# A scan and a gated MLP on one core: a table made on the chip, and another order of the first loads

## The chip, the cores and the metric

The kernel runs on one NeuronCore of a Trainium2 chip. The metric is device time in microseconds (us) of one execution. The core has five engines with instruction streams of their own: TensorE (PE in the profile, with its weight loads as PEld), VectorE (DVE), ScalarE (ACT), GpSimd (POOL) and SyncE (SP), which here only issues DMAs. Each engine works through its stream in order and waits on semaphores for the others. DMAs are carried out by 16 DMA engines that all queues share.

## The reference

Two stages. The first is a causal linear attention with decays, for 4 batches, 8 heads, 768 positions, head size 32 and state size 16; the second is a gated MLP on the 3072 resulting rows of 256.

```python
log_a = np.log(np.clip(a, 1e-06, 1.0))
for c in range(nc):                                   # chunks of the sequence
    cum = np.cumsum(la, axis=-1)
    L = np.exp(cum[:, :, :, None] - cum[:, :, None, :]) * causal
    M = np.einsum('bhin,bhjn->bhij', Cc, Bc) * L
    y_intra = np.einsum('bhij,bhjd->bhid', M, xc)
    y_inter = np.einsum('bhin,bhnd->bhid', Cc, state) * np.exp(cum)[:, :, :, None]
    state = decay_full * state + sum over j of Bc * xc * decay_from_j
g = x @ w_gate                                        # (3072, 256) @ (256, 1536)
out = (g * (1.0 / (1.0 + np.exp(-g))) * (x @ w_val)) @ w_out
```

## The kernel before, in words

**Blocks.** The sequence is cut into NB = 6 blocks of 128 positions, each of K = 2 pieces of Q = 64. A block holds T = 512 rows of the MLP (4 batches by 128). Block by block, the attention gives y, which is the input x of the MLP; TensorE then runs the gate and value products (tile gv, 12 column pieces f of 128) and later the sums over the hidden size (tile po).

**Decay tables.** L[j, i] is the product of decays from position j to position i. It is made on VectorE by a scan along i: state = state * a + d, where d is a table with a one at i = j, which starts the product. This diagonal table is the tile dj, 128 partitions (j, twice 64) by 8 heads by W = 65. dn is the like table for E, the decays from the start of a piece. For block 0 the decays come as 8 rows (load_rows), are clipped on VectorE (clip_rows), spread over 128 partitions by TensorE matmuls with a table pick (spread, tile a), and scanned from PSUM (scan_spread). For later blocks all decays are loaded once (load_all), clipped on GpSimd (clip_all), written to DRAM (write_all, tile clipped) and read back as broadcasts (load_aj into L, load_an into E).

**Attention of a block.** heads_apart makes Cz from C on ScalarE or VectorE with masks hm out of the constants cs; scores (tile S) are matmuls of B and Cz; mix multiplies L by S on VectorE; weigh_first and weigh_b multiply B, which lies beside x in the tile xb, by the last column of L; sums gives the states (tile st), apart puts them into T; values and carried give y; weigh_c multiplies C by E. For block 0, x_whole copies y to the tile xf.

**Weights.** The weights come as float64 bit patterns, 18 pieces of 512 KB (12 of gate and value, wg0 to wg11, then 6 of the output, wo0 to wo5), and are turned into float32 on the chip: w_magnitude and w_rest on ScalarE, w_range on GpSimd (on VectorE for pieces 1 and 2), then w_shift, w_sign and w_round on VectorE. The raw pieces lie in 8 buffers (RAW = 8, tag wraw), which the hidden tiles hh use too; a buffer comes free when its piece is rounded. In block 0 the products use the rounded piece as float32; for later blocks w_high, w_minus and w_low split it into two parts.

**The order.** Nothing but the opening statements (from load_rows to the fills of dn) is in hand order. All else is an operation in a list: add(engine, cost, run, rank, needs, takes, uses, gives, lag). A planner (class Plan) runs through modelled time at build time: on each engine it takes, among the operations that can start first, the one of lowest rank. What it finds is the program order of each engine. lag is the modelled transfer time of a load, needs are operations that must come before, and follow(list) fixes an order of issue. ScalarE and VectorE are chosen by the planner where both are given with a cost. The plan's times only decide the order; on the chip engines wait on semaphores.

In the plan before, the raw pieces 2 and 3 are issued behind the scores of block 0, 4 and 5 behind mixes 1 and 3, and 7 behind y of block 0. VectorE's opening order is fixed as the scans of block 0, mixes 0 to 2, the weighing of B (bt), mix 3, E, the weighing of C (ce) and the sign step of piece 0.

All engine calls go through a helper (class Ordered), so every operation of the profile has the line L191; they are told apart by their tiles.

## Time and profile before

| | |
|---|---|
| median of 3 runs | 351.83 us (351.35 to 351.98) |
| the profiled execution | 352.14 us, its span 350.3 us |
| TensorE busy | 342.8 us, 98% of the span |
| VectorE busy | 231.3 us, 66% |
| ScalarE busy | 121.9 us, 35% |
| GpSimd busy | 46.0 us, 13% |
| DMA | 31.28 MB, mean 89 GB/s |
| first gate and value product of block 0 | starts at 16.89 us |

How to read it: rows of a timeline give the start in us, the busy time in us, engine, line, operation, output tile <- input tiles, shape and count (xN are N instructions merged), and in brackets the idle time ahead of it with what ended it. SPq, ACTq and POOLq are DMA issues; the time of such a row is that of the issue, not of the transfer. A row of the DMA view gives a load, its queue, its size and the median us from issue to landing. A row of the waits gives total us, times, longest. A row of the windows gives the stretch, its length, the busy time and count of PE, PEld, DVE, ACT and POOL, the granted TensorE clock, the DMA share and GB/s. Busy time of a matmul is modelled at its end, so neighbours overlap in the rows.

### The profile page before, as it was taken

To read this page: it belongs to the slowest core of one execution; us is meant where nothing else is said; L and a number is where in the kernel's file an instruction comes from. 1 tells how busy PE (TensorE), PEld (TensorE's weight loads), DVE (VectorE), ACT (ScalarE), POOL (GpSimd) and SP (SyncE) were. 2 spreads that over 40 slices of the span, in tenths; PEclk is the share of its full clock that TensorE was granted. 3 is DMA by queue.
4 is the path that set the end of the run, shared out by engine and by line. 5 is a ranking of instruction groups with operands and counts; after the bars stand their busy time and mean duration, and the time that the engine had idled before them with its cause. 6 is when DMAs were issued, how large, how long until landed. Compare 5 with 4: busy or idle time off the path is not lost.

```text
span 350.3 us, 7386 instructions
## 1 busy us (share of the span) xinstructions
PE 342.8 (98%) x3183; PEld 265.6 (76%) x3184; DVE 231.3 (66%) x415; ACT 121.9 (35%) x221; POOL 46.0 (13%) x36
## 2 busy tenths in 40 slices
PE   7999989999999999999999999999999999999996
PEld 5644445688878888878888878888888888888895
DVE  4999999998689774686447677456676430565320
ACT  3599677434355512212222222221212221222221
POOL 1374884402301000000000000000000000000000
PEclk9999999999999999999999999999999999999999
DMA  7799998850000751000382000281000000100001
GB/s 258 241 318 309 334 277 185 225 120 2 1 2 4 204 158 62 0 2 2 111 175 82 0 2 2 84 199 59 24 3 2 2 2 0 60 2 0 0 2 60
DMA packets 10216, 31.28 MB, mean 89 GB/s; under 512 B 1184, under 2 KB 2080, under 8 KB 9544
## 3 DMA queue, kind: packets, MB, share of 16 engines
q1 hardware_dynamic: 8136, 26.77, 25.4%
q0 software_dynamic: 1728, 3.15, 5.0%
q10 hardware_dynamic: 320, 0.89, 0.8%
q8 instruction: 25, 0.41, 0.5%
q14 instruction: 7, 0.06, 0.1%
HBM read 24.32 MB, written 3.35 MB: 79 GB/s over the span
## 4 chain that ended last, share of the span: by engine, by line
PE 92%; DVE 3%; issue 1%; ACT 0%; DVEq 0%; ACTq 0%
PE gv L191 57%; PE po L191 28%; PE y L191 5%; PE S L191 2%; DVE wg8w L191 1%; DVE L L191 1%; DVE wg0w L191 1%; DVE E L191 0%; DVE wg7w L191 0%; DVE sg L191 0%; DVE xb L191 0%; ACT ob L191 0%; DVE bc L191 0%; DVEq L191 0%; ACTq L191 0%
## 5 line engine op out<-in xcount | busy, mean ns | idle before, releaser
L191 DVE TENSOR_TENSOR sg<-gv,sg 128x512 f32<-128x512 f32 x72 | 49.5, 688 | 66.5 <-PE gv L191 65.3
L191 ACT ACTIVATE sg<-gv 128x512 f32<-128x512 f32 x72 | 43.1, 598 | 109.7 <-PE gv L191 109.6
L191 DVE TENSOR_TENSOR hh<-sg,hh 128x512 fp32r<-128x512 f32 x72 | 49.5, 691 | 16.0 <-ACT hh L191 14.6
L191 ACT CAST hh<-sg 128x512 fp32r<-128x512 f32 x36 | 22.3, 623 | 31.1 <-PE po L191 17.5
L191 DVE TENSOR_TENSOR_SCAN L<-L,dj 128x520 f32<-128x520 f32 x20 | 23.9, 1228 | 5.8 <-DMA L<-clipped 5.8
L191 ACT COPY ob<-po 128x512 f32<-128x512 f32 (+1 forms) x13 | 7.2, 555 | 48.6 <-PE po L191 48.2
L191 DVE CAST hh<-sg 128x512 fp32r<-128x512 f32 x36 | 15.8, 438 | 1.2
L191 PE MATMUL po<-hh,wo4h 128*128 128x512 f32 (+1 forms) x52 | 15.2, 375 | 0.0
L191 PE MATMUL po<-hh,wo2h 128*128 128x512 f32 (+1 forms) x52 | 15.2, 375 | 0.0
L191 PE MATMUL po<-hh,wo0h 128*128 128x512 f32 (+1 forms) x52 | 15.2, 375 | 0.0
L191 DVE TENSOR_TENSOR L<-S,L 128x512 f32<-128x512 f32 x24 | 15.1, 678 | 0.0
L191 PE MATMUL po<-hh,wo5h 128*128 128x512 f32 (+1 forms) x52 | 15.1, 373 | 0.0
L191 PE MATMUL po<-hh,wo1h 128*128 128x512 f32 (+1 forms) x52 | 15.0, 373 | 0.0
L191 PE MATMUL po<-hh,wo3h 128*128 128x512 f32 (+1 forms) x52 | 15.0, 373 | 0.0
L191 PEld LDWEIGHTS y<-L,xb 64*32 64x32 f32 x768 | 9.6, 111 | 3.1 <-issue 1.8
L191 PE MATMUL y<-L,xb 64*32 64x64 f32 x768 | 11.9, 239 | 0.0
L191 PEld LDWEIGHTS po<-hh,wo0h 128*128 128x128 f32 x52 | 9.5, 188 | 1.9 <-issue 0.2
L191 PEld LDWEIGHTS po<-hh,wo5h 128*128 128x128 f32 x52 | 9.5, 188 | 1.7
L191 PEld LDWEIGHTS po<-hh,wo1h 128*128 128x128 f32 x52 | 9.5, 188 | 1.7
L191 PEld LDWEIGHTS po<-hh,wo3h 128*128 128x128 f32 x52 | 9.5, 188 | 1.7
L191 PEld LDWEIGHTS po<-hh,wo2h 128*128 128x128 f32 x52 | 9.4, 188 | 1.8
L191 PEld LDWEIGHTS po<-hh,wo4h 128*128 128x128 f32 x52 | 9.4, 188 | 1.7
(304 smaller groups left out, 756.0 us busy)
## 6 DMA issues: line engine op xcount, KB each, us to landing
L<-clipped SPq DMA_DIRECT2D x10, 520.0 KB, 10.7
xb<-in_xb SPq DMA_DIRECT2D x5, 768.0 KB, 13.8
bc<-in_bc SPq DMA_DIRECT2D x6, 512.0 KB, 4.4
out<-ob SPq DMA_DIRECT2D x11, 256.0 KB, 2.0
E<-clipped SPq DMA_DIRECT2D x5, 260.0 KB
xb<-in_xb ACTq DMA_DIRECT2D x1, 768.0 KB, 6.3
wg0r<-in_wgv SPq DMA_DIRECT2D x1, 512.0 KB
wg1r<-in_wgv SPq DMA_DIRECT2D x1, 512.0 KB
```

What stands on the lines that cost most here:

```text
L191: ins = getattr(self.engine, name)(*a, **k)
```

## The change

**The table dj** is no longer copied from the constants. Two iotas on GpSimd (one for each 64 partitions) write i - j into a new tile step_of, and one VectorE instruction compares it with 0 into dj. Both stand ahead of the other opening work of their engines' planned order: the iotas ahead of the fills of unit and dn, the compare ahead of the clipping of the rows. The constants cs shrink by 65 columns of 131 (from 65.5 KB by half).

**The loads.** x and B of block 0 (load_xb) go out on SP behind C and B (load_bc) where they went out on ScalarE's queue. The raw pieces lose their needs on scores, mixes and y. A new list ORDER fixes the order of issue on SP: piece 7, the write of the clipped decays, piece 8, block 1's bc, aj and xb, piece 9, block 1's an, piece 10. The modelled lags of several loads change.

**The order of VectorE's opening** now puts the weighing of B ahead of all four mixes, and the rounding of piece 0 behind its sign step. All four copies x_whole are ScalarE's. The rest step of piece 3 comes behind the last of them.

```diff
--- before.py
+++ after.py
@@ -219,7 +219,8 @@
     ps_at = pool("ps_at", 4, space=PSUM)
 
     cs = const.tile([P, CST], F32, name="cs")
-    eye, hm, blk = cs[:, 0:W], cs[:, W : W + 2], cs[:, W + 2 : W + 2 + 2 * D]
+    hm, blk = cs[:, :2], cs[:, 2 : 2 + 2 * D]
+    step_of = const.tile([P, W], F32, name="step")
     pick = const.tile([64, BATCH + 1, P], F32, name="pick")
     dj = const.tile([P, H, W], F32, name="dj")
     dn = const.tile([P, BATCH * K, W], F32, name="dn")
@@ -285,7 +286,7 @@
     def load_xb(k):
         t = bl[k]["xb"] = att.tile([P, BATCH, DM + P], F32, tag="xb", name=f"xb{k}")
         bl[k]["x"], bl[k]["Bj"] = t[:, :, :DM], t[:, :, DM:]
-        (sp if k else se).dma_start(t, xb[k])
+        sp.dma_start(t, xb[k])
 
 
     def clip(t):
@@ -664,7 +665,7 @@
 
         if not i:
             rest[n] = ps_at.tile([P, 512], F32, tag="at", name=f"rest{n}")
-        times, wide = (4, 64) if not n else (1, 512)
+        times, wide = ((4, 64), (1, 512))[n]
         for _ in range(times):
             te.matmul(rest[n][:, :wide], unit[:, :P], unit[:, :wide], start=True, stop=True)
 
@@ -678,6 +679,12 @@
     load_all()
     ve.memset(warm, 1.0)
     se.activation(warm, warm, AF.Silu)
+    for q in range(K):
+        ge.iota(
+            step_of[piece(q)], pattern=[[1, W]], base=0, channel_multiplier=-1,
+            allow_small_or_imprecise_dtypes=True,
+        )
+    ve.tensor_scalar(dj, step_of.unsqueeze(1).to_broadcast([P, H, W]), 0.0, None, ALU.is_equal)
     ge.memset(unit[:, P:], 1.0)
     ge.memset(dn, 0.0)
     ge.memset(dn[:, :, :1], 1.0)
@@ -709,7 +716,6 @@
         return begin_sum[k] + f * PO
 
     add("-", 0.0, lambda: None, -9, gives="pick", lag=0.1)
-    add([("Act", 0.6), ("DVE", 0.6)], None, lambda e: copy(e, dj, eye.unsqueeze(1).to_broadcast([P, H, W])), -8.5, ["cs"], gives="dj")
     add("-", 0.0, lambda: None, -8, gives="cs", lag=0.4)
 
 
@@ -722,12 +728,12 @@
 
     for i in range(NW):
         r = due(0, i) - 1.0 if i < NF else due_sum(0, 2 * (i - NF)) - 1.0
-        add("SP", 0.48, do(w_fetch, i), r - 9.0, [("S", 0, BATCH - 1)] if i in (2, 3) else [("M", 0, 2 * i - 7)] if i in (4, 5) else [("y", 0)] if i == 7 else [], takes=[("raw", ("raw", i))], gives=("raw", i), lag=2.1)
+        add("SP", 0.48, do(w_fetch, i), r - 9.0, takes=[("raw", ("raw", i))], gives=("raw", i), lag=1.3)
         add("Act", 0.57, do(w_magnitude, i, "Act"), r - 5.5, [("raw", i)], takes=[("sg" if i < NF else "w", ("w", i))], gives=("mag", i))
         far = not 0 < i < 3
         e, c = ("Pool", 2.2) if far else ("DVE", 0.335)
         add(e, c, do(w_range, i, ge if far else ve), r - 4.5, [("mag", i), *([("round", i - 1)] if i == 1 else [])], gives=("range", i))
-        add("Act", 0.57, do(w_rest, i, "Act"), r - 4.5, [("raw", i)], gives=("rest", i))
+        add("Act", 0.57, do(w_rest, i, "Act"), r - 4.5, [("raw", i), *([("xf", 3)] if i == 3 else [])], gives=("rest", i))
         add("DVE", 0.335, do(w_shift, i), r - 4.2, [("range", i)], gives=("shift", i))
         add("DVE", 0.6, do(w_sign, i), r - 3.9, [("shift", i)], gives=("sign", i))
         add("DVE", 0.6, do(w_round, i), r - 3.3, [("sign", i), ("rest", i)], uses=[("raw", i)], gives=("round", i))
@@ -744,7 +750,7 @@
 
     add("-", 0.0, lambda: None, -7.9, gives="all", lag=0.9)
     add("Pool", 1.0, clip_all, -9, ["all"], gives="clipped")
-    add("SP", 0.48, write_all, -9, ["clipped"], gives="written", lag=0.9)
+    add("SP", 0.48, write_all, -9, ["clipped"], gives="written", lag=1.5)
 
 
     for k in range(NB):
@@ -764,8 +770,8 @@
         def load(f):
             return do(f, k) if k else lambda: None
 
-        add(*q, load(load_bc), FETCH["bc"] if k == 1 else z - 7 if k else -7.7, late + behind("bc") + loaded, takes=[("bc", BC)], gives=("bc", k), lag=2.1)
-        add(*q, load(load_xb), FETCH["xb"] if k == 1 else z - 6 if k else -6, late + behind("xb") + loaded, takes=[("xb", XB)], gives=("xb", k), lag=3.1)
+        add(*q, load(load_bc), FETCH["bc"] if k == 1 else z - 7 if k else -7.7, late + behind("bc") + loaded, takes=[("bc", BC)], gives=("bc", k), lag=1.3)
+        add(*q, load(load_xb), FETCH["xb"] if k == 1 else z - 6 if k else -6, late + behind("xb") + loaded, takes=[("xb", XB)], gives=("xb", k), lag=1.9)
         if not k:
             add("-", 0.0, lambda: None, -9, takes=[("x", "rows")], gives="rows", lag=0.2)
             for i in range(3):
@@ -775,12 +781,12 @@
                 for i in range(2 if b < BATCH else 1):
                     t = ("spread", b, i)
                     add("PE", 0.25 if first(b, i) else 0.45, do(spread, b, i), r + 0.5 * i, [("clip", b % 2 if b < BATCH else 2), "pick"], takes=[("mm" if first(b, i) else "at", t)], uses=[t, "rows"], gives=t, kind="s")
-                    need = [t, ("decays", 0), "dj"] + ([("scan0", b)] if i else [])
+                    need = [t, ("decays", 0)] + ([("scan0", b)] if i else [])
                     done = ("E", 0) if b == BATCH else ("L", 0, b) if i else ("scan0", b)
                     add("DVE", 0.63, do(scan_spread, b, i), r + 0.5 * i, need, uses=[t], gives=done)
         else:
             add("SP", 0.96, do(load_aj, k), FETCH["aj"] if k == 1 else z - 12, ["written", ("decays", k), *late], gives=("aj", k), lag=4.3)
-            add("SP", 0.48, do(load_an, k), FETCH["an"] if k == 1 else z - 9, ["written", ("decays", k), *late], gives=("an", k), lag=1.1)
+            add("SP", 0.48, do(load_an, k), FETCH["an"] if k == 1 else z - 9, ["written", ("decays", k), *late], gives=("an", k), lag=2.4)
             for b in range(BATCH):
                 add("DVE", 1.14, do(scan_j, k, b), z + 0.5 + b, [("aj", k)], gives=("L", k, b), slack=1.0)
             add("DVE", 1.17, do(scan_n, k), z + 6, [("an", k)], gives=("E", k), slack=1.0)
@@ -830,7 +836,7 @@
         if not k:
             add("-", 0.0, new_whole, -9, [("clip", 2)], takes=[("x", "xf")], gives="xf")
             for i in range(2 * K):
-                add([("Act", 0.36)] if i < 3 else [("Act", 0.36), ("DVE", 0.36)], None, do(x_whole, i), -1 + i / 10, [("vals", i) if i < 2 else ("y", 0), "xf", *([("round", 0)] if i == 3 else [])], uses=[y[i]], gives=("xf", i))
+                add([("Act", 0.36)], None, do(x_whole, i), -1 + i / 10, [("vals", i) if i < 2 else ("y", 0), "xf"], uses=[y[i]], gives=("xf", i))
             continue
         add("-", 0.0, do(new_x, k), z + 15, [("x", k - 1)] if k > 1 else ["xf"], takes=[("x", ("x", k))], gives=("x", k))
         for i in range(2 * K):
@@ -878,18 +884,20 @@
         ("spread", BATCH, 0), *(("st", 0, b) for b in range(BATCH)),
     ])
     plan.follow([("raw", i) for i in range(NW)])
-    plan.follow([("L", 0, b) if i else ("scan0", b) for b, i in halves] + [("M", 0, p) for p in range(3)] + [("bt", 0)] + [("M", 0, 3), ("E", 0), ("ce", 0), ("sign", 0)])
+    plan.follow(ORDER)
+    plan.follow([("L", 0, b) if i else ("scan0", b) for b, i in halves] + [("bt", 0)] + [("M", 0, p) for p in range(NP)] + [("E", 0), ("ce", 0), ("sign", 0), ("round", 0)])
     plan.STAY = {"Act": 0.0, "PE": 0.3}
     plan.issue()
 
 
-CST = W + 2 + 2 * D
+CST = 2 + 2 * D
 NA = NB * K * BATCH * H // P
 IDLE = [-9.0] * 6, [0.5, 1.0]
 IDLE_AFTER = [], [("y", 0)]
 FETCH = dict(aj=10.0, an=35.0, bc=12.0, xb=31.0)
 LATER = 3.0
 PAGE = 4.4
+ORDER = [("raw", 7), "written", ("raw", 8), ("bc", 1), ("aj", 1), ("xb", 1), ("raw", 9), ("an", 1), ("raw", 10)]
 LEAD = {1: -30.0, 2: -44.0, 3: -44.0}
 LATE = {2: NF + 2}
 
@@ -922,10 +930,9 @@
 
     p = np.arange(P)
     cst = np.zeros((P, CST), np.float32)
-    cst[:, :W] = (p % Q)[:, None] == np.arange(W)[None, :]
     odd = (p // N) % 2
-    cst[:, W : W + 2] = odd[:, None] == np.arange(2)[None, :]
-    cst[:, W + 2 : W + 2 + 2 * D] = odd[:, None] == (np.arange(2 * D) // D)[None, :]
+    cst[:, :2] = odd[:, None] == np.arange(2)[None, :]
+    cst[:, 2 : 2 + 2 * D] = odd[:, None] == (np.arange(2 * D) // D)[None, :]
     m = np.arange(BATCH * P)
     own = (np.arange(H)[:, None] == BATCH * (m % P // Q) + m // P).astype(np.float32)
     own = f(np.concatenate([own, np.arange(H)[:, None] == p // N], axis=1).astype(np.float32))
```

## The prediction

> **What bounds the kernel now.** I read the page first (busy times and the 40 slices), then the chain that ended last in order of time, then the waits of the first 64 us, and then the timeline of each engine up to 50 us.
>
> ```profile
> PE 342.8 (98%) x3183; PEld 265.6 (76%) x3184; DVE 231.3 (66%) x415; ACT 121.9 (35%) x221; POOL 46.0 (13%) x36
> ...
> DVE  4999999998689774686447677456676430565320
> ...
> 59.61 38.00 PE gv L191 x156
> ```
>
> TensorE is busy for 98% of the span, so no more than 7.5 us (350.3 - 342.8) could be saved without taking matmuls away. From 59.61 on the chain is TensorE work with no gap that could be given back. What this change can move lies ahead of 16.89, where the first gate/value product of block 0 begins, and in the one pause of TensorE after it:
>
> ```profile
> 47.08 3.67 PE L191 MATMUL gv<-xf,wg8w 128*128 128x512 f32 x8 [1.15 <-DVE wg8w L191]
> ```
>
> Before 16.89 VectorE sets the pace. Its work there, with the TensorE work that feeds it:
>
> ```profile
> 3.46 0.86 DVE L191 TENSOR_SCALAR rows<-rows 8x512 f32<-8x512 f32 x2 [2.45 <-DMA rows<-in_aj]
> 5.72 1.88 DVE L191 TENSOR_TENSOR_SCAN L<-a,dj 128x260 f32<-128x260 f32 x3 [1.40 <-ACT dj L191]
> 7.70 3.04 DVE L191 TENSOR_TENSOR_SCAN L<-a,dj 128x260 f32<-128x260 f32 x5
> 10.67 1.85 DVE L191 TENSOR_TENSOR L<-S,L 128x512 f32<-128x512 f32 x3
> 12.45 0.67 DVE L191 TENSOR_TENSOR xb<-xb,L 128x512 f32<-128x512 f32 x1
> 14.76 0.42 DVE L191 TENSOR_SCALAR wg0w<-wg0w 128x512 int32<-128x512 int32 x1
> 16.05 0.69 DVE L191 CUSTOM_DVE_ANT_0 wg0w<-wg0r,wg0w 128x1024 uint16<-128x1024 uint16 x1
> 16.66 0.42 DVE L191 COPY xf<-y 128x256 f32<-128x256 f32 x1
> 3.93 4.28 PE L191 MATMUL a<-rows,pick 8*128 8x260 f32 x16 [1.40 <-DVE rows L191]
> 8.13 2.30 PE L191 MATMUL S<-Cz,bc 32*64 32x128 f32 x64
> 16.89 3.67 PE L191 MATMUL gv<-xf,wg0w 128*128 128x512 f32 x8 [0.40 <-DVE wg0w L191]
> ```
>
> The row to see is the second: VectorE stood for 1.40 us because the diagonal table dj was still being copied. From 5.72 it works without a gap that anything but itself makes, up to the rounding of piece 0 (16.05), and the first product follows that by 0.84.
>
> **The change, part by part.**
>
> *Diagonal table on the chip.* Removed: the ScalarE copy and its wait for the constants.
>
> ```profile
> 5.07 0.63 ACT L191 COPY dj<-cs 128x520 f32<-128x520 f32 x1 [1.03 <-DMA cs<-in_cst]
> 1.09 0.71 POOL L191 MEMSET dn<- 128x520 f32 x2
> 8.96 1.49 POOL L191 TENSOR_SCALAR all<-all 128x384 f32<-128x384 f32 x1 [7.16 <-DMA all<-in_an]
> ```
>
> Added: two iotas (64x65) at the head of GpSimd and one compare of 128x520 at the head of VectorE, which stands ahead of the clipping at 3.46 in VectorE's order. No row shows an iota. It is bounded by two GpSimd fills of a wider tile, 0.71 for the pair, and by two of GpSimd's 128x384 arithmetic, 2 x 1.49 = 2.98. GpSimd starts at 0.74 (1.09 less the fill ahead of it, some 0.35), so the ramp is there between 1.5 and 3.7. The compare is nearest to the 128x512 TENSOR_SCALAR at 14.76, 0.42. The table is then ready at 2.0 to 4.2, against clipping at 3.46: a cost of 0 to 0.75. I take 0, since 65 columns are nearer to a fill; VectorE's 2.45 us of waiting for the rows hides it. The fills pushed back on GpSimd are dn, first read by the E scan near 13, and part of unit, read at 16.
>
> The gain is not the whole 1.40. A scan also needs its spread. The 16 matmuls of the spreads start (4.28 - 0.64)/15 = 0.24 apart, each 0.64 long:
>
> ```profile
> L191 PE MATMUL a<-rows,pick x18: 636/636/797, 3.9 to 11.0; 8*128 8x260 f32 x18
> ```
>
> so the first spread (two matmuls) ends at 3.93 + 0.24 + 0.64 = 4.81, and the first scan can start at about 4.9: 0.8 earlier. Scans run 0.60 apart, spreads 0.49, so after the first no scan waits for a spread, and they end near 9.9 instead of 10.74.
>
> *Order behind the scans.* The weighing of B (12.45) now stands before the four mixes, where it stood after three. The mixes need the scores, which TensorE ends at 8.13 + 2.30 = 10.43; they come behind the spreads, and these don't move. So VectorE scans to 9.9, weighs B to 10.5 in what would else be a gap, and begins mixing at about 10.6. From 10.67 to 16.89 there were 6.22 us with the weighing inside; without its 0.60 it is 5.62: the first product starts at 10.6 + 5.62 = 16.2, **0.7 us earlier**. If the scores came sooner the bound would be VectorE alone: 0.8; with the dearest ramp it is 0. TensorE's side agrees: the last mix ends 0.67 earlier, and vals, carried and the copies of y follow it. The fourth copy (0.42 on VectorE at 16.66) goes to ScalarE, which did the others in 0.39; it ends near 16.2, and the products that read it come a third of a piece later, so it costs nothing, and VectorE saves some 0.4 there.
>
> *x behind C and B on one queue.* Both loads now go out on SP.
>
> ```profile
> 2.05 0.45 ACTq L191 DMA_DIRECT2D xb<-in_xb  x1
> xb<-in_xb ACTq DMA_DIRECT2D x1, 768.0 KB, 6.3
> 10.00:16.00 6.00, 5.93 (x240) 4.28 (x230) 5.78 (x11) 3.24 (x9) 2.37 (x2) 1.00 0.60 175
> 16.00:22.00 6.00, 5.60 (x25) 2.47 (x19) 5.92 (x14) 5.99 (x12) 2.75 (x2) 1.00 1.07 422
> ```
>
> (last two columns: DMA share and GB/s). C and B stop sharing with x, which helps ScalarE but not the scores, bound by the spreads. x was there at 2.05 + 6.3 = 8.4. It now has no weight piece ahead of it, and is first wanted at 9.9. Cost 0, while it takes less than 7.6 us from an issue near 2.3. The decays to be clipped and piece 0, behind it on SP, go out one issue (0.45 us) later; piece 0 is wanted by VectorE only at 14.76 - 0.7, so that is hidden by the mixes.
>
> *Pieces not held back.* Six more issues of about 0.43 us on SP before the write of the clipped decays. Between 10 and 16 the DMA engines moved 175 GB/s and 422 right after, so the hold left (422 - 175) x 6 us = 1.5 MB, near three pieces, unmoved. Everything behind comes up to 3.5 us earlier, and pieces 7 and 8 more, as they no longer stand behind the second block's loads.
>
> *Decays and the second block behind pieces 7 and 8.* The queue is now 7, write, 8, bc, aj, xb, 9, an, 10. Piece 8 waits for the buffer of piece 0, whose rounding ends near 16, about where the second block's C and B went out before.
>
> ```profile
> 16.27 0.33 SPq L191 DMA_DIRECT2D bc<-in_bc  x1
> 16.70 1.15 SPq L191 DMA_DIRECT2D L<-clipped  x2
> L<-clipped SPq DMA_DIRECT2D x2, 520.0 KB, 12.9
> 32.53 2.36 DVE L191 TENSOR_TENSOR_SCAN L<-L,dj 128x520 f32<-128x520 f32 x2
> ```
>
> The second half of the aj broadcast, issued 0.6 behind the first, landed at 17.3 + 12.9 = 30.2; its scans started at 32.53, 2.3 us of slack. Two more pieces stand ahead of it (1 MB, 2.5 us at 422 GB/s) against 3.5 us won: no cost. Now the pause at 47.08:
>
> ```profile
> wg8r<-in_wgv SPq DMA_DIRECT2D x1, 512.0 KB, 16.8
> 37.06 0.66 ACT L191 ACTIVATE wg8w<-wg8r 128x512 f32<-128x512 f32 x1
> 38.27 3.18 POOL L191 TENSOR_SCALAR wg8w<-wg8w 128x512 f32<-128x512 f32 x1
> 41.02 0.68 DVE L191 TENSOR_TENSOR L<-S,L 128x512 f32<-128x512 f32 x1
> 45.24 1.09 DVE L191 TENSOR_TENSOR bc<-bc,E 128x512 f32<-128x512 f32 x1
> 46.25 0.68 DVE L191 CUSTOM_DVE_ANT_0 wg8w<-wg8r,wg8w 128x1024 uint16<-128x1024 uint16 x1
> 47.79 0.68 DVE L191 TENSOR_TENSOR L<-S,L 128x512 f32<-128x512 f32 x1
> 50.68 0.80 PE L191 MATMUL y<-xb 64*32 64x64 f32 x60
> ```
>
> Piece 8 was 16.8 us on its way, and ScalarE took it at 37.06. GpSimd clamped it to 41.45, and VectorE did two mixes (0.68 each) and the weighing of C (1.09) of the second block ahead of its rounding, 2.4 us that are wanted only near 50.7. With piece 8 there 10 us earlier its rounding (planner's rank 39.7) goes ahead of these (41 to 44.5): it ends at 46.93 - 2.4 - 1.1 (the earlier start and the copy) = 43.4, where TensorE arrives at 45.93 - 0.7 = 45.2. The pause goes: **1.15 us**. Bounds: 0, if the planner's order stays; nothing above 1.15, as there is no other pause. What is late next: the last mix ended at 48.47 and was wanted at 50.68; VectorE's total is unchanged and 1.1 earlier, the want 1.85 earlier, so 1.4 us of slack remain.
>
> Sum: 0.7 + 1.15 = 1.85 us. The profiled execution took 352.14 (span 350.3), which becomes 350.3. It lies 0.31 above the median of the runs, 351.83; against that median I forecast **350.0 us**.
>
> **Rivals.**
>
> *The pause stays or moves.* VectorE is full in every slice from 5 to 70 us, so an order that serves the rounding of 8 earlier may leave another piece late. For it: those full slices; against it: 59.61 on shows no pause, and the one at 47.08 is the only one ahead of it. Only 0.7 is left: 351.1.
>
> *More at the start.* If the scores also end earlier, because C and B are there sooner and the banks are freed sooner, and ScalarE is free, the whole 1.4 arrives: 351.83 - 1.4 - 1.15 = 349.3. Against it: TensorE's spreads end at 8.2 as before.
>
> *TensorE's clock.* The same 64 score matmuls took 2.30 us at 8.13 and, in the second block, half:
>
> ```profile
> 37.66 1.21 PE L191 MATMUL S<-Cz,bc 32*64 32x128 f32 x64
> 20.40 3.60 PE L191 MATMUL gv<-xf,wg1w 128*128 128x512 f32 x8
> ```
>
> The granted clock is 1.00 in the windows shown from 10 to 22, so that record doesn't say it, but the array ran at about half pace early on. At 16.89 this was over (piece 0 was busy for 3.67, piece 1 for 3.60). If the pace rises at the same time as before, 0.8 us of products at half pace cost 0.4: 350.4. If a whole piece runs so, it costs (20.40 - 16.89) x (2.30/1.21 - 1) = 3.2: 353.2. [...]
>
> *Slower: x late.* The weighing of B stands first behind the scans, so VectorE, and everything behind it in order, waits for x. Six pieces are now issued right behind x. If the loads in flight share the engines instead of following each other, x is late. Each us past 9.9 goes to the first product in full; from 9.9 + 1.85 = 11.75, a landing of 9.4 us, the kernel is slower than before. Priced by the second block's x, which took 15.2 us among many loads: 2.3 + 15.2 - 9.9 = 7.6 later, less 1.85: 357.6; by the 7.0 of piece 4, nothing. For it: those 15.2; against it: piece 4, issued right behind piece 3, took 2.2 us longer, so they followed each other.
>
> ```profile
> wg3r<-in_wgv SPq DMA_DIRECT2D x1, 512.0 KB, 4.8
> wg4r<-in_wgv SPq DMA_DIRECT2D x1, 512.0 KB, 7.0
> xb<-in_xb SPq DMA_DIRECT2D x1, 768.0 KB, 15.2
> ```
>
> **How the numbers follow.** Forecast 0.47; pause stays 0.23; more at the start 0.10; clock 0.10; x late (with a slow ramp beside it) 0.10. The measurement can tell about 0.2%, 0.7 us, from no change: 351.13 to 352.53 counts as the same. The case of the pause sits on that edge and is split, 0.12 and 0.11; the clock is split 0.04, 0.03, 0.03; of the forecast 0.03 falls inside the edge. Faster: 0.44 + 0.10 + 0.12 + 0.04 = 0.70; same: 0.03 + 0.11 + 0.03 = 0.17; slower 0.13. The range 349.2 to 351.9 takes in the first three cases and the mild clock.
>
> **What would show it.** First scan at about 4.9 with its wait on a spread; dj ready before 3; mixes at 10.6, the first product at 16.2; x landed before 9.9; no low DMA rate between 10 and 16; piece 8 landed before 27, its rounding before 45, and no wait on it; aj landed near 30. I am wrong if VectorE waits for GpSimd ahead of 3.46, for x near 10, or if TensorE pauses elsewhere before 64.

## The result and the profile after

| | before | after |
|---|---|---|
| median of 4 runs each, same chip | 351.90 us (351.35 to 352.82) | 356.33 us (355.64 to 357.73) |
| ratio after / before | | 1.0127, 95% interval 1.0108 to 1.0146 |
| profiled execution, its span | 352.14, 350.3 us | 355.64, 353.9 us |

The change makes the kernel **slower by 1.3%**; 350.0 was forecast. The profiled execution is the fastest of the four after, so the traces show 3.6 us of the 4.4 between the medians.

The page of after, its busy times and the rows of its DMA queues (packets, MB, share of 16 engines):

```profile
PE 343.1 (97%) x3183; PEld 265.3 (75%) x3184; DVE 229.1 (65%) x412; ACT 123.0 (35%) x224; POOL 46.7 (13%) x38
...
q8 instruction: 25, 0.41, 0.5%
```

TensorE's busy time is nearly what it was (342.8), so what was lost is waiting. The waits of TensorE after, without the two of its first 4 us (total us, times, longest):

```profile
PE y L191 <- issue: 2.6, 1, 2.6
PE gv L191 <- ACT sg L191: 1.3, 1, 1.3
...
PE y L191 <- ACT T L191: 0.6, 1, 0.6
PE gv L191 <- DVE sg L191: 0.3, 1, 0.3
PE gv L191 <- ACT xf L191: 0.3, 1, 0.3
```

None of these was there before; the one on wg8w is gone. The first is the largest, and "issue" means that nothing in the profile releases TensorE there.

**Up to 12.9 us all goes as forecast.** The timelines of GpSimd and VectorE after:

```profile
0.85 0.42 POOL L191 IOTA step<- 64x65 f32 x2 [0.40 <-POOLq L941]
```

```profile
1.30 0.73 DVE L191 TENSOR_SCALAR dj<-step 128x520 f32<-128x520 f32 x1 [0.29 <-POOL step L191]
...
4.95 1.88 DVE L191 TENSOR_TENSOR_SCAN L<-a,dj 128x260 f32<-128x260 f32 x3 [0.89 <-PE a L191]
...
10.00 0.69 DVE L191 TENSOR_TENSOR xb<-xb,L 128x512 f32<-128x512 f32 x1
10.61 2.48 DVE L191 TENSOR_TENSOR L<-S,L 128x512 f32<-128x512 f32 x4
...
15.20 0.68 DVE L191 CUSTOM_DVE_ANT_0 wg0w<-wg0r,wg0w 128x1024 uint16<-128x1024 uint16 x1
```

The table is ready at 2.03, the first scan starts at 4.95 behind a spread, the weighing finds x there at 10.00, the mixes start at 10.61. Piece 0 is rounded at 15.88, 0.86 earlier than before (16.74). So VectorE would have let the first product start near 16.1.

**Then TensorE stops.** Its timeline after:

```profile
11.93 0.98 PE L191 MATMUL y<-L,xb 64*32 64x64 f32 x50
15.53 1.39 PE L191 MATMUL y<-L,xb 64*32 64x64 f32 x77 [2.62 <-issue]
...
18.77 3.76 PE L191 MATMUL gv<-xf,wg0w 128*128 128x512 f32 x8 [0.25 <-ACT xf L191]
```

In the middle of the first values, between the 50th and the next of 127 like matmuls in a row, it stands still for 2.62 us. Their last input, the last mix on VectorE, was there at 13.09 (10.61 + 2.48), 2.4 us before it goes on. The first product starts at 18.77 where it had started at 16.89. Before, TensorE went through the same stretch without a gap:

```profile
11.52 1.62 PE L191 MATMUL y<-L,xb 64*32 64x64 f32 x64
13.17 1.16 PE L191 MATMUL st<-xb 64*32 64x64 f32 x63
```

What was different around it shows in windows of 1 us (stretch, its length, busy time and count of PE, PEld, DVE, ACT, POOL, granted clock, DMA share, GB/s), first before, then after:

```profile
10.00:11.00 1.00, 1.00 (x16) 0.52 (x6) 1.00 (x3) 0.90 (x2) 0.60 (x2) 1.00 0.06 25
```

```profile
10.00:11.00 1.00, 1.00 (x7) 0.34 (x8) 1.00 (x2) 1.00 (x2) 0.61 (x2) 1.00 1.05 430
...
13.00:14.00 1.00, 0.00 (x0) 0.00 (x0) 1.00 (x4) 1.00 (x5) 0.00 (x0) 1.00 0.97 389
```

Before, the DMA engines were nearly idle from 10 to 11; after, they are full. On them travels one packet that is nobody's data: a 16 KB one of the queue "q8 instruction". The DMA queues in the 0.1 us from 11.0 before, and in the 0.1 us from 12.9 after:

```profile
q8 instruction: 1, 0.02, 58.2%
```

```profile
q8 instruction: 1, 0.02, 69.2%
```

A share is of 16 engines in 0.1 us, so the packet took 0.582 x 1.6 = 0.93 us before and 1.11 after. Before it runs from 11.07 to 12.00, after from 12.96 to 14.07, and TensorE goes on 1.46 later. The reading taken here is that the queue carries TensorE's program in pages, on the DMA engines that carry the weights. It has 25 packets and 0.41 MB in a run, and TensorE has 3183 matmuls and 3184 weight loads, 6367 instructions, so some 255 to a packet. e4 and the counts under "All runs side by side" test this reading.

**Why the engines were idle before** isn't what the prediction supposed. SP's issues, first before, then after:

```profile
4.69 0.43 SPq L191 DMA_DIRECT2D wg1r<-in_wgv  x1
10.47 0.39 SPq L191 DMA_DIRECT2D clipped<-all  x1
10.91 1.49 SPq L191 DMA_DIRECT2D wg2r<-in_wgv  x1
```

```profile
8.49 0.33 SPq L191 DMA_DIRECT2D wg7r<-in_wgv  x1
10.16 0.39 SPq L191 DMA_DIRECT2D clipped<-all  x1
15.95 0.34 SPq L191 DMA_DIRECT2D wg8r<-in_wgv  x1
```

The write of the clipped decays waits for GpSimd, and before it stood ahead of piece 2 in SP's order: that, not a wait on scores or mixes, kept pieces 2 to 6 back. (The needs only had a part in the order: without them, in e2, pieces 2 and 3 stand ahead of the write.) The change sets the write behind piece 7.

**Where the rest went.** The start of products on TensorE:

| | before | after | difference |
|---|---|---|---|
| block 0, piece 0 | 16.89 | 18.77 | +1.88 |
| scores of block 1 | 37.66 | 39.63 | +1.97 |
| block 0, piece 8 | 47.08 | 47.74 | +0.66 |
| block 0, piece 9 | 52.32 | 52.85 | +0.53 |
| block 0, piece 10 | 55.85 | 57.82 | +1.97 |
| block 0, piece 11 | 61.36 | 64.11 | +2.75 |
| block 1, piece 0 | 64.40 | 67.14 | +2.74 |
| block 1, piece 5 | 78.41 | 81.95 | +3.54 |
| end of the span | 350.3 | 353.9 | +3.6 |

Rows of TensorE's timeline, before and then after:

```profile
52.32 3.70 PE L191 MATMUL gv<-xf,wg9w 128*128 128x512 f32 x8
55.85 1.88 PE L191 MATMUL gv<-xf,wg10w 128*128 128x512 f32 x4
```

```profile
47.74 3.60 PE L191 MATMUL gv<-xf,wg8w 128*128 128x512 f32 x8
...
52.85 3.70 PE L191 MATMUL gv<-xf,wg9w 128*128 128x512 f32 x8
57.82 1.98 PE L191 MATMUL gv<-xf,wg10w 128*128 128x512 f32 x4 [1.26 <-ACT sg L191]
60.41 0.86 PE L191 MATMUL y<-L,xb 64*32 64x64 f32 x64 [0.61 <-ACT T L191]
...
80.45 0.73 PE L191 MATMUL gv<-xh,wg4h 128*128 128x512 f32 x2 [0.33 <-DVE sg L191]
```

The pause at piece 8 goes, as forecast, and gives 1.31 back. Behind it 2.94 is lost again. Three new pauses hold 2.20 of that (1.26, 0.61 and 0.33); the other 0.74 has no wait of its own in the rows. Two of the pauses are ScalarE's, which stands for the last raw piece with the work that TensorE wants behind it in its order; the third is VectorE's, which stands for block 2's decays and then its x:

```profile
56.10 0.67 ACT L191 ACTIVATE wo5r<-wo5r 128x512 int32<-128x512 uint32 x1 [4.39 <-DMA wo5r<-in_wo]
```

```profile
73.46 2.38 DVE L191 TENSOR_TENSOR_SCAN L<-L,dj 128x520 f32<-128x520 f32 x2 [0.99 <-DMA L<-clipped]
...
77.97 0.69 DVE L191 TENSOR_TENSOR xb<-xb,L 128x128 f32<-128x128 f32 x3 [0.41 <-DMA xb<-in_xb]
```

Together: 1.97 at the start, -1.31 at piece 8, 2.94 behind it, 3.60.

### The profile page after: what moved, and what is told of

Its sections match the earlier page's. It is cut to its first block, busy times and chain, and to the rows that moved or that the text cites. A ratio compares the mean times of both kernels' runs of the same rounds, so it can differ in the third digit from the quotient of the medians.

```text
span 353.9 us, 7384 instructions
## 1 busy us (share of the span) xinstructions
PE 343.1 (97%) x3183; PEld 265.3 (75%) x3184; DVE 229.1 (65%) x412; ACT 123.0 (35%) x224; POOL 46.7 (13%) x38
## 4 chain that ended last, share of the span: by engine, by line
PE 80%; DVE 8%; DMA 6%; ACT 2%; issue 2%; POOL 1%; DVEq 0%; ACTq 0%; SPq 0%
PE gv L191 44%; PE po L191 28%; PE y L191 4%; DMA xb<-in_xb 3%; DMA wo5r<-in_wo 2%; PE S L191 2%; DVE L L191 2%; PE a L191 2%; DVE sg L191 1%; DMA rows<-in_aj 1%; POOL wo1w L191 1%; DVE wg9w L191 1%; DVE wg4w L191 0%; DVE wg3w L191 0%; DVE wg8w L191 0%
## 5 line engine op out<-in xcount | busy, mean ns | idle before, releaser
L191 ACT CAST hh<-sg 128x512 fp32r<-128x512 f32 x33 | 20.6, 623 | 33.0 <-PE po L191 21.1
L191 DVE CAST hh<-sg 128x512 fp32r<-128x512 f32 x39 | 16.6, 426 | 2.4 <-PE po L191 1.2
```

Of the source, the lines that this page charges most:

```text
L191: ins = getattr(self.engine, name)(*a, **k)
```

## The experiments

**The theory:** with the DMA engines full, TensorE's page comes late, and that stop is the loss at the start. **Its rivals:** a page takes a fixed time, and TensorE now only reaches the end of one sooner; TensorE waits for data that the profile doesn't name; the modelled lags, which order ScalarE and VectorE, make the loss; the table or the new order of VectorE makes it. A second question is what the early pieces are worth behind 40 us.

### e1: the needs of the pieces put back

```diff
-  do(w_fetch, i), r - 9.0, takes=...
+  do(w_fetch, i), r - 9.0, [("S", 0, BATCH - 1)] if i in (2, 3) else [("M", 0, 2 * i - 7)] if i in (4, 5) else [], takes=...
```

> The changed kernel with one thing put back: pieces 2 and 3 wait for the scores, 4 and 5 for mixes 1 and 3 (piece 7 not for y). Theory A (TensorE's program comes in pages by the same DMA engines, and a page that is asked for while they are full of weight pieces comes late): TensorE's stop of 2.62 us in the first values shrinks to under 0.5 us, the page's packet starts near 11 instead of 12.96, the first gate/value product starts near 16.2 instead of 18.77, and the time falls by 2 to 2.6 us to about 353.7. Rival B (a page takes a fixed time, and TensorE now reaches its end sooner): the stop stays above 1.5 us and the time within 1 us of 356.3. Rival C (the stop is a wait for x or for a bank): the stop stays.

Measured: 355.81 us, ratio 1.014 (1.0075 to 1.0204). SP's order and the DMA rate near 10 us (402 to 426 GB/s from 10 to 11) stayed as after, and so did a stop of 1.95 us. The edit held nothing: needs only order the program, and SP's program came out the same. It doesn't test the theory; it showed where the hold of before really was.

### e2: the kernel before without the needs of its pieces

```diff
-  do(w_fetch, i), r - 9.0, [("S", 0, BATCH - 1)] if i in (2, 3) else ... [("y", 0)] if i == 7 else [], takes=...
+  do(w_fetch, i), r - 9.0, takes=...
```

> The kernel before with one thing taken: no raw piece is held back behind scores, mixes or y. Theory A: the page packet that started at 11.07 starts 1 to 3 us later, TensorE stops for 1 us or more between 12 and 15 with no releaser shown, the first product starts at 18 to 19 instead of 16.89; the time rises by 1 to 2 us (the 1.15 us pause at piece 8 may go). Rival B: no stop, first product at 16.9 or earlier, time 350.5 to 351.9.

Measured: 352.84 us, ratio 1.0021 (1.0000 to 1.0042). SP's issues and TensorE's timeline:

```profile
5.78 0.44 SPq L191 DMA_DIRECT2D wg3r<-in_wgv  x1
10.82 0.39 SPq L191 DMA_DIRECT2D clipped<-all  x1
```

```profile
14.73 0.35 PE L191 MATMUL st<-xb 64*32 64x64 f32 x7 [1.05 <-issue]
17.94 4.13 PE L191 MATMUL gv<-xf,wg0w 128*128 128x512 f32 x8 [0.22 <-issue]
```

Two pieces more ahead of the write are enough to make the stop appear in the old kernel, with the old table and VectorE's old order. The first product starts 1.05 later than before. The pause at piece 8 was gone here too (47.28), so the end is nearly even.

### e3: the pieces' modelled lag put back

```diff
-  takes=[("raw", ("raw", i))], gives=("raw", i), lag=1.3)
+  takes=[("raw", ("raw", i))], gives=("raw", i), lag=2.1)
```

> The changed kernel with one thing put back: the planner reckons with 2.1 us of transfer for a raw piece, not 1.3. Theory A2 (beside the page, the second loss is that ScalarE's steps of a piece are planned ahead of its landing, so that ScalarE stands for 4.4 us at wo5 and TensorE for 1.26 and 0.61 behind it): these two pauses go, the 2.62 us stop stays (over 2 us), the time falls by 1 to 2 us to about 354.7. Rival (piece wo5 is late by the queue, whatever the plan): the pauses stay and the time stays within 0.5 us.

Measured: 356.70 us, ratio 1.0142 (1.0122 to 1.0163). The pauses on wo5's copy and on T went, as the lag theory expected, but a stop of 1.88 stayed, VectorE's L and sg made TensorE wait 0.9 and 1.5 elsewhere, and the first product ran slowly (4.71 us to the next one, where before took 3.51). The time is no better, where 354.7 was expected: the lag changes which piece ScalarE or VectorE stands for.

### e4: 18 of the 24 warming matmuls left out

```diff
-        times, wide = ((4, 64), (1, 512))[n]
+        times, wide = ((1, 64), (1, 512))[n]
```

No result depends on these matmuls; they only keep TensorE busy at the start (1.46 us from 1.06 on, in after).

> The changed kernel with 6 of TensorE's 24 warming matmuls at the start, so 18 matmuls with their weight loads (36 instructions) fewer ahead of the scan; no result depends on them. Theory A and B (the stop is the end of a page of program): the stop comes 18 matmuls later, behind all 64 of the first values and about 4 of the next group. Rival C (a wait for data or a bank): the stop stays behind the 50th matmul of the first values. The time may change by the array's clock, up to 2 us.

Measured: 354.01 us (a single time, without an interval). TensorE's timeline:

```profile
11.79 1.68 PE L191 MATMUL y<-L,xb 64*32 64x64 f32 x68
15.46 1.14 PE L191 MATMUL y<-L,xb 64*32 64x64 f32 x59 [1.99 <-issue]
```

The stop stands after the 68th of the same 127 matmuls, where after had it behind the 50th: 18 fewer matmuls ahead, 18 later. A wait on data would have stayed at its matmul. The stop belongs to a place in the program, counted in instructions.

### e5 and e6: the write of the clipped decays ahead of piece 2, in both kernels

e5, from after:

```diff
-ORDER = [("raw", 7), "written", ("raw", 8), ...]
+ORDER = [("raw", 1), "written", ("raw", 2)], [("raw", 7), ("raw", 8), ...]
```

e6, from e2:

```diff
     plan.follow([("raw", i) for i in range(NW)])
+    plan.follow([("raw", 1), "written", ("raw", 2)])
```

> The changed kernel with the write of the clipped decays put between pieces 1 and 2 on SP (its wait for GpSimd, to about 10.2, holds pieces 2 to 7 back as before), where it stood behind piece 7. Theory A (page of TensorE's program behind weight pieces): DMA idle near 10 to 11, page packet starts by 11 instead of 12.96, the stop of 2.62 us falls under 0.5, first product at 16.0 to 16.6 instead of 18.77, time 2 to 3 us under the changed kernel, 353.3 to 354.3; what is left over the kernel before are the later pauses behind ScalarE (wo pieces) and the second block's loads. Rival B (fixed page time, TensorE is earlier): stop stays over 1.5 us, time near 356.

> The kernel before without the planner's hold-backs, but with the write of the clipped decays still between pieces 1 and 2. Theory A: no stop in the states (1.05 us without the write there), first product at 16.9 as before, and the pause at piece 8 stays away, since piece 7 and 8 come earlier: 350.5 to 351.2, 0.7 to 1.4 us under the kernel before. Rival B: stop near 1 us, time near 352.8.

Measured: 358.56 us, ratio 1.0185 (1.0152 to 1.0217), and 356.42 us, ratio 1.0133 (1.0111 to 1.0154). In both the page packet came at 10 us (table below) and the stop near 13 was gone: the theory's step held. Both times missed what was expected (353.3 to 354.3 and 350.5 to 351.2) and were worse than the kernels they were made from. In e5 ScalarE now stood for the held piece 2 ahead of the copies of y, and TensorE for ScalarE:

```profile
18.18 5.40 PE L191 MATMUL gv<-xf,wg0w 128*128 128x512 f32 x8 [2.35 <-ACT xf L191]
```

That product took 5.40 us, as the granted clock is 0.50 in the windows from 19 to 22.

In e6 the first product started at 16.43 and piece 8 at 46.18, 0.9 ahead of before; then the same kind of stop came at another page, in the values of block 1, and behind it the granted clock was 0.50 from 56 to 59:

```profile
55.73 0.31 PE L191 MATMUL y<-L,xb 64*32 64x64 f32 x1 [2.35 <-issue]
```

```profile
56.00:57.00 1.00, 1.00 (x3) 0.48 (x3) 1.00 (x5) 1.00 (x4) 0.15 (x1) 0.50 1.14 213
```

(Last columns: clock 0.50, DMA share 1.14, 213 GB/s.) That page's packet came at 53.37; before, at 50.39, with no stop.

### e7 and e8: the table on the chip alone, and with e6

e7 is before with the hunks of the change that make dj from step_of, and none of the others; e8 adds the two edits of e6.

```diff
+        ge.iota(step_of[piece(q)], ...)
+    ve.tensor_scalar(dj, step_of..., 0.0, None, ALU.is_equal)
-    add([("Act", 0.6), ("DVE", 0.6)], None, lambda e: copy(e, dj, eye...), -8.5, ["cs"], gives="dj")
-                    need = [t, ("decays", 0), "dj"] + ...
+                    need = [t, ("decays", 0)] + ...
```

> The kernel before with the diagonal table made on the chip and nothing else. Prediction's step: first scan near 4.9, first product 0.5 to 0.8 earlier than 16.89, no stop beyond 0.5 us, pause at piece 8 as before, time 351.1 to 351.4. Rival (TensorE reaches the end of its page 0.7 us sooner and waits for it there, or its clock rises no sooner): the first piece's products end no earlier, time 351.8 to 352.

> The kernel before with both: the table on the chip, and no hold-backs with the write between pieces 1 and 2. If the two steps add as the prediction said (0.7 and 1.15): 350.0 to 350.4. If only one holds: 350.7 to 351.3. If the page sets the start whatever VectorE does: as the run without the table.

Measured: e7 351.64 us, ratio 0.9999 (0.9985 to 1.0013); e8 353.94 us, ratio 1.0082 (1.0043 to 1.0120). e7's timeline:

```profile
16.04 3.67 PE L191 MATMUL gv<-xf,wg0w 128*128 128x512 f32 x8
...
46.75 3.67 PE L191 MATMUL gv<-xf,wg8w 128*128 128x512 f32 x8 [1.55 <-DVE wg8w L191]
```

In this trace the first product is 0.85 earlier than in the one of before, and most of it is handed back at piece 8, which comes when it comes: the pause grows from 1.15 to 1.55, and piece 8 starts only 0.33 earlier. The time stays the same, where 351.1 to 351.4 was expected. The table is not the cause of the loss.

How much of the 0.85 is the table's is another matter. In e7 VectorE clips the rows 0.41 earlier (3.05, before 3.46), as they landed sooner. And e6 and e8 differ by the table alone: e6, which still copies it, has its first scan at 5.24 and waits there for the spread, not for the copy; e8 has it at 5.16. Their first products start at 16.43 and 16.42. Over all traces the first scan starts at 5.72, 5.17 and 5.24 in the three kernels that copy the table (before, e2, e6), and at 4.81 to 5.16 in the twelve that make it. So the wait of 1.40 in before is in good part one execution in which the constants came late.

e8 (piece 8 at 45.86) then has a stop in block 1's values again, of 0.96, and is far from the 350.0 to 351.3 expected.

### e9, e12 and e14: the table, and pieces 7 and 8 ahead of part of block 1's loads

On top of e7, with pieces 2 to 5 held as before. e9 takes away piece 7's need on y as well:

```diff
+    plan.follow([("raw", 7), ("raw", 8), ("bc", 1), ("aj", 1), ("xb", 1), ("raw", 9), ("an", 1), ("raw", 10)])
```

e12 moves only piece 8 ahead of block 1's x:

```diff
+    plan.follow([("raw", 8), ("xb", 1)])
```

> The kernel before with the table on the chip, and pieces 7 and 8 ahead of the second block's loads on SP (bc, aj, xb, then 9, an, 10); all else as before, write between pieces 1 and 2, x on ScalarE's queue. Theory A with L: first product at 16.0 as with the table alone, pause at piece 8 (1.6 us with the table alone) gone, time 349.9 to 350.6. Rival (the pause only moves, to a page of program or to the second block's loads): 351 to 352.5 with a pause of 1 us or more between 45 and 65.

> The kernel before with the table on the chip and only piece 8 put ahead of the second block's x and B (0.77 MB), which stood ahead of it. Theory A with L: piece 8 lands some 2 us sooner, its pause falls from 1.6 to under 0.5, time 350.3 to 351.0. Rival (the pause is VectorE's own load, not piece 8's landing): pause stays over 1 us, time as with the table alone, 351.6.

Measured: e9 353.75 us, ratio 1.0058 (1.0029 to 1.0087); e12 351.47 us, ratio 0.9987 (0.9972 to 1.0002). In both the pause at piece 8 is gone. In e9 there follow 0.49 on piece 9 and a stop of 0.94 in block 1's values; its rival was right in kind, as the pause moved, but the time is above the rival's 352.5. e12 has only a stop of 0.19 there (at 51.40), and leads by 1.78 at block 1's first product (62.62); then VectorE stands for block 2's decays, with a product of sg behind them in its order that TensorE needs:

```profile
44.97 3.60 PE L191 MATMUL gv<-xf,wg8w 128*128 128x512 f32 x8
...
62.62 1.03 PE L191 MATMUL gv<-xh,wg0h 128*128 128x512 f32 x2
...
73.79 0.73 PE L191 MATMUL gv<-xh,wg3h 128*128 128x512 f32 x2 [1.03 <-DVE sg L191]
```

```profile
70.78 2.37 DVE L191 TENSOR_TENSOR_SCAN L<-L,dj 128x520 f32<-128x520 f32 x2 [2.02 <-DMA L<-clipped]
```

In this trace a lead of the size forecast is there at 62 us. At block 1's piece 4 it is 75.69 - 75.28 = 0.41, and 0.4 at the end of the span (349.9 against 350.3): 1.03 went in this pause, and some 0.3 around it. So e14 changes only what the planner believes of that load, from e12; SP's order stays the same, and VectorE's scans of block 2 move behind two products of sg and the rounding of wo2:

```diff
-  ["written", ("decays", k), *late], gives=("aj", k), lag=4.3)
+  ["written", ("decays", k), *late], gives=("aj", k), lag=11.0 if k == 2 else 4.3)
```

> The kernel e12 (table on the chip, piece 8 ahead of block 1's x) with the modelled transfer time of block 2's decays at 11.0 instead of 4.3. SyncE's order of issue is the same as in e12; VectorE's order puts two hh steps, wo1l, two sg products and the rounding of wo2 ahead of the first scan of block 2. Theory that e12's lead of 1.73 us at block 1's piece 3 is lost only because sg stands in VectorE's order behind a scan that waits for a load (VectorE waited 2.0, TensorE 1.03): the wait of TensorE on sg near 73.8 goes, block 1's piece 5 starts near 76.7 (before 78.41), and the time is 1.2 to 1.7 us below the kernel before, near 350.2, ratio 0.996. Rival, that the lead has no use since block 2's loads set the pace behind it: the first product of block 2 or its scores wait instead, TensorE pauses by 1 us or more between 80 and 110, and the time stays at 351.5 or above.

Measured: 351.12 us (before beside it 352.00), ratio 0.9971 (0.9955 to 0.9987). Its timelines of TensorE and VectorE:

```profile
63.18 1.02 PE L191 MATMUL gv<-xh,wg0h 128*128 128x512 f32 x2
...
77.20 0.62 PE L191 MATMUL gv<-xh,wg5h 128*128 128x512 f32 x2
```

```profile
75.22 1.24 DVE L191 TENSOR_TENSOR_SCAN L<-L,dj 128x520 f32<-128x520 f32 x1
```

The scan no longer waits, nor does TensorE for sg, and the lead of 64.40 - 63.18 = 1.22 at block 1's first product is still 1.21 at its piece 5 (78.41 there before) and 1.2 at the end of the span (349.1). In this execution the lead at block 1 was smaller than in e12: the first product started later (16.32 against 16.09), and at 51.96 TensorE stopped for 0.43 where e12 had stopped for 0.19. The time fell by 0.88, less than the 1.2 to 1.7 that was expected. It is the only kernel of the study whose interval lies below the one before, by 0.3%.

### e10 and e11: all modelled lags put back, without and with the write ahead of piece 2

e10 is after with the lags of before (raw 2.1, bc 2.1, xb 3.1, an 1.1, written 0.9):

```diff
-add("SP", 0.48, write_all, -9, ["clipped"], gives="written", lag=1.5)
+add("SP", 0.48, write_all, -9, ["clipped"], gives="written", lag=0.9)
```

and so on; e11 adds the split ORDER of e5.

> The changed kernel with all modelled transfer times of the planner put back (raw pieces 2.1, bc 2.1, xb 3.1, an 1.1, the write 0.9); the loads go out in the order of the change. Theory L (the second half of the loss is that shorter modelled times put steps of ScalarE and VectorE ahead of loads that then are not there): no wait of ScalarE on a wo piece and of VectorE on the third block's loads over 1 us, TensorE's pauses between 50 and 85 gone, while the stop near 13 stays (1.5 us or more); time 353.3 to 354.7. Rival (the loads come late by the queue's order, whatever the plan): pauses stay, time 355.5 or more.

> As the run before in this call, and the write of the clipped decays put between pieces 1 and 2. Theory A with L: the page's packet starts by 11, no stop near 13, no wait for xf at the first product (ScalarE has no weight step ahead of it that waits), first product near 16.1, pause at piece 8 gone by the early pieces 7 and 8: 349.9 to 351.2, faster than the kernel before. If ScalarE's wait for pieces in front of xf comes from the hold itself, not from the modelled times: first product at 18 again, 353 or more.

Measured: 358.13 us, ratio 1.0168 (1.0131 to 1.0205), and 358.17 us, ratio 1.0177 (1.0143 to 1.0210). e10 keeps a stop of 1.8 near 13, so the lags aren't the cause of that stop. The pauses between 50 and 85, which theory L expected to go, don't go either: TensorE waits 2.03 for piece 9, and the granted clock behind that wait is 0.50 from 54 to 56. e11's edit differs from e10's by the write alone; its stop near 13 is gone, the first product starts at 16.37 and piece 8 at 45.24, and it loses all of that again, 1.08 on piece 9 and 2.44 in block 1's values, where the page is late. Its 349.9 to 351.2 was far off:

```profile
55.88 0.27 PE L191 MATMUL y<-L,xb 64*32 64x64 f32 x2 [2.44 <-issue]
```

### All runs side by side

The first page packet of each run, the stop behind it, and the start of the first product and the time from there to the next one:

| kernel | packet of q8 | stop near 13 to 15 | first product, to the next |
|---|---|---|---|
| before | 11.07 to 12.00 | none | 16.89, 3.51 |
| after | 12.96 to 14.07 | 2.62 | 18.77, 3.60 |
| e1 | 12.48 to 13.59 | 1.95 | 18.19, 4.06 |
| e2 | 12.21 to 13.24 | 1.05 | 17.94, 3.97 |
| e3 | 12.17 to 13.25 | 1.88 | 17.87, 4.71 |
| e4 | 13.02 to 14.13 | 1.99 | 18.45, 4.05 |
| e10 | 12.36 to 13.36 | 1.79 | 18.00, 4.12 |
| e6 | 10.07 to 11.06 | none | 16.43, 3.50 |
| e7 | 9.94 to 11.04 | none | 16.04, 3.55 |
| e8 | 10.83 to 11.78 | none | 16.42, 3.51 |
| e9 | 9.98 to 11.12 | none | 16.52, 3.56 |
| e11 | 9.94 to 11.22 | none | 16.37, 3.51 |
| e12 | 9.72 to 10.81 | none | 16.09, 3.51 |
| e14 | 9.92 to 11.21 | none | 16.32, 3.52 |

(e5 has its packet from 9.99 to 10.99 and no stop; its first product is late for ScalarE, above.) Every kernel that keeps the write ahead of piece 2 gets its page by 12.0 and doesn't stop there; every kernel that sends pieces past it gets it after 13.2 and does. From 10 to 11 the DMA engines move 25 to 189 GB/s in the first kind, and 410 to 430 in the second. The edits of the pairs e2 and e6, and e10 and e11, differ in the place of the write alone; the planner then moves some later issues too. After a stop the first product runs slower too, by 0.1 to 1.2 us.

**Counting matmuls** in the traces settles more than the times do. In all six kernels with a stop near 13, it lies behind TensorE's 221st matmul, whatever that works on: values in after, states in e2. The later stops (e6, e8, e9, e10, e11, and the short ones of e12 and e14) lie behind the 597th to 599th. All thirteen end 1.24 to 1.50 us after their packet. The nine kernels that don't stop at the 221st go past it 1.51 to 2.35 us after theirs. That is what a wait for the packet would give; a wait for data would follow the operation, not the count.

It also answers the rival of the fixed time. In the nine, the packet starts when 104 to 106 matmuls have begun, in the six when 165 to 221 have, so it is late by the program too. And e5 and e11 go past the 221st matmul at 12.62 and 12.73, as early as after gets there (12.60), and don't stop. The late packets took 1.00 to 1.11 us and the others 0.93 to 1.28, so it is their start that is late.

Full engines alone don't make a stop. The next packet of before starts at 17.80, at 426 GB/s and with a DMA share of 1.06 from 17 to 18, and nothing stops. TensorE is in products of 512 columns there, some 0.44 us each (3.51 for eight); at 11.52 it went through 64 values in 1.62 us, some 0.025 each, and so came to the end of its page soon.

## Why the prediction was wrong

**Diagonal table on the chip: right in its costs, lucky in its gain.** First scan forecast at 4.9, measured 4.95; the ramp, bounded by 0.71 and 2.98 for the pair, took 0.42, below both; the compare 0.73, where 0.42 was taken, beside waiting that hid it. But the gain was read off one execution, in which the constants came late: its copy starts at 5.07, that of e2 at 4.52 and that of e6 at 4.25. Beside e6 the table gained 0.08 at the first scan and 0.01 at the first product (e8), and e7's median is nearly that of before.

**Order behind the scans: right on VectorE.** Mixes at 10.61 as forecast, piece 0 rounded 0.86 earlier. The scores ended at 9.88 and not at 10.43, so VectorE alone set this pace, which is the prediction's bound of 0.8. The copies of y, though, costed at nothing, now stand behind other work on ScalarE: TensorE waits 0.25 for the last, in the row at 18.77.

**x behind C and B: right.** x was there at 10.00, so the rival in which it comes late, the one that ended slower, is wrong. The kernel is slower for another reason.

**Pieces not held back: this step failed.** It counted the 1.5 MB that fit into the gap from 10 to 16 as pure gain, read the gap as unused, and put the cost to TensorE at nothing. TensorE's own program used it: its page crossed the idle engines from 11.07 to 12.00. With the gap filled, the page is late and TensorE stands for 2.62, which eats the 0.7 and 1.88 more. None of the prediction's rivals names this: it gave 0.13 to a slower kernel, for a late x and a slow clock. The prediction had looked at the DMA queues for loads only; the row of q8 was on the page of before with the same 25 packets. It also took the needs for waits; what held the pieces was the write's place on SP.

**Decays and second block behind pieces 7 and 8: half right.** The pause at piece 8 went, worth 1.31 in after (1.15 forecast). "Nothing above, as there is no other pause" and the 1.4 us of slack behind it were wrong: 2.94 was lost again behind it, most of it in three other places. In e12 the pause is gone and the lead at 62 us is 1.78; e9, e11 and after show what can follow, and e14 that the lead is kept where VectorE's order no longer puts a scan that waits ahead of what TensorE needs. Its rival, that the pause moves, was right in kind (0.23), but it was priced at the loss of 1.15, and 2.94 was lost.

**TensorE's clock** was a rival as a shift of the start, at 0.4 or 3.2 us. It came as something that follows a stop. The clock records of the traces begin, at full clock, between 13.97 and 16.77 in the nine kernels without the early stop, and between 18.93 and 20.27 in the six with it; the windows ahead of them (up to 15.90 in before, 18.93 in after) show 1.00 only because nothing is on record there. TensorE is slower until then: the warming matmul of 512 columns (tile rest) took 0.61 at 17.91 in after, as in e1 to e4, and 0.39 at 16.10 in before. The first product is slower too, which costs 0.1 in after and 0.5 to 1.2 in e1 to e4 and e10 (3.60 and 3.97 to 4.71 to the next one, where before took 3.51). In three traces the record also falls to half about when a longer wait ends, for some 3.4 us each time (0.83 on average from 50 to 60 in e6 and e10, 0.94 and 0.89 from 10 to 20 and 20 to 30 in e5): behind waits of 2.35 in e5, 2.35 in e6 and 2.03 in e10. Behind the wait of 2.44 in e11 it doesn't (1.00 from 50 to 60). What brings such a stretch on, and what sets its length, no run shows.

**What stays open.** No run moved the page without moving other loads, and why its start is late, a turn behind other packets or something else, wasn't tried. Single runs of e8, e9 and e11 lie 4 to 5 us apart. The longest have a mean granted clock of 0.989 to 0.995 and the others 0.998 to 1.0, so stretches at half clock are likely part of it. One of 3.4 us at 0.50 loses 1.7 us, by estimate; the rest has no cause here. And the pauses behind 48 us in after depend on the order that the planner gives ScalarE and VectorE as well as on the loads; e3 and e10 show that the modelled lags move them about, and e14 undoes one such pause, but in the kernel with the held pieces. Whether after itself can be mended in this way wasn't tried.

## What to carry to other kernels

A stretch in which the DMA engines stand idle isn't free room (here it held TensorE's page, and filling it moved that from 11.07 to 12.96 and cost a stop of 2.62 us): see what crosses them there, the "instruction" queue too, before filling it, and place long bursts of loads so that a gap falls where TensorE is due its next page in the middle of short matmuls. (That last was not tried in after itself.) In a queue that works in order, look up which issue ahead really waits; a load can be held by its neighbour and not by its own conditions, as wg2r was (issued at 10.91, behind the write at 10.47). And where one pause is removed late in a chain that is 98% busy, price the next waits behind it (the last raw weight, the next block's loads) at more than nothing: here 1.31 came back at piece 8, and 2.94 was lost behind it.

## What the runs showed of the hardware

As e4 and the counts bear out, TensorE's program comes in packets of 16 KB over the same DMA engines as the loads: 25 for its 6367 instructions, about one for 255. Where the engines had room at 10 us (25 to 189 GB/s from 10 to 11) the packet came in time and TensorE went on without a gap. Where they were full from 10 to 12 (406 to 430 GB/s) it came 1.1 to 3.3 us later (12.17 to 13.02 against 9.72 to 11.07), and TensorE stood for 1.05 to 2.62 us at a place that is fixed by the count of instructions (e4, and the 221st matmul of all six). It went on 1.33 to 1.50 us after the packet's end. With full engines, too, one packet came with no stop, at 17.80 in before (426 GB/s from 17 to 18), where TensorE was in products of some 0.44 us each.
